# A thinned fold, evictions on another engine and four moved table mends in the prologue of a fused FNet and MLP-Mixer kernel

## Chip, cores and metric

The kernel runs on one core of one Trainium2 chip. The metric is the device time of one execution in microseconds (us), and lower is better.

## The reference

It takes an FFT over the sequence and the features, keeps the real part, and puts an MLP-Mixer behind it (first over tokens, then over channels). Batch 8, sequence 3008, width 256, all float32:

```python
x = np.fft.fft(np.fft.fft(x, axis=1), axis=2).real       # 8 x 3008 x 256
h = np.maximum(x.transpose(0, 2, 1) @ w_tok1, 0.0) @ w_tok2   # 3008 -> 256 -> 3008
u = x + h.transpose(0, 2, 1)
out = u + np.maximum(u @ w_ch1, 0.0) @ w_ch2             # 256 -> 1536 -> 256
```

## The kernel before

It is already tuned: TensorE is fed almost without a gap from batch 1 on, and what follows happens in the first 76 us. There the tables are built, batch 0 goes through its transform, and batch 1 is prepared between batch 0's matmuls. Names that the text needs:

- `xp`, `xm`: rows of x and the mirrored rows. GpSimd issues their loads; the last two of a batch are gathers.
- `fold`: sums and differences of `xp` and `xm` (fold 0 is that of batch 0, fold 1 that of batch 1; tiles `fa`, `fb`, `sab`, `eo`, last `pad`), the input of the transform's first stage `pz` -> `z`. The second stage `pw` -> `w` uses table `td`, then comes `py` -> `yt`.
- tok1 (`pt`, with tables `hp` and `hq`) and tok2 (`pu`, added to `yt` into `ut`): the token part. `pc` -> `c`, `po` or `pa`/`pb` -> `osb`: the channel part, with `s`, sums of `c` that feed `pa` and `pb`. A *slot* is one 128-column block of the first channel product; twelve slots make a chunk of 512 tokens.

GpSimd issues the large loads in program order between its own arithmetic. VectorE does fold 0 and fold 1 and shares the evictions of PSUM with ScalarE. The four *mends* set three columns of `td` right:

```python
    # GpSimd: index columns, the mirror table `anti`, then the weight loads
    for k in range(2):
        ts(ixc[:, k:k + 1], cfeat[:], 128.0 + 0.5 * k, AT.add, 2.0, AT.mult, eng=G)
    # ... tables on VectorE and ScalarE ...
    ts(acol[:], pcol[:], -1.0, AT.mult, 127.0, AT.add, eng=G)
    ts(anti[:], jrow[:, 0:P], acol[:], AT.is_equal, eng=G)

    def load_wc1(k):
        c = slice(HC * k, HC * k + HC)
        for q in range(2):
            gdma(wc1[64 * q:64 * q + 64, 0, c],
                 dram(wc1_t, q * DCH + HC * k, [[2 * DCH, 64], [1, HC]]))
        gather(wc1[:, 1, c], dram(wc1_t, 0, [[HC, 2 * D], [1, HC]]), ixc[:, k:k + 1])

    def load_rest():
        load_wc1(0)
        for th in range(2):
            gdma(w2n[:, th, :], dram(w2_t, th * P * S, [[S, P], [1, S]]))
        load_wc1(1)
        gdma(wc2[:, :, 0:D], dram(wc2_t, 0, [[D, P], [P * D, NCT], [1, D]]))

    # ... the order of the prologue ...
    load_rest()
    fold0 = fold(0, V)
    filler(12)
    take(fold0, 5)                       # first half of fold 0, on VectorE
    ts(ol[:, 0:1], ol[:, 0:1], 2.0, AT.mult)                             # the four mends
    ts(td[:, 0:1], td[:, 64:65], 0.5, AT.mult, ol[:, 0:1], AT.add)
    ts(td[:, 65:66], td[:, 64:65], 0.5, AT.mult, ol[:, 0:1], AT.subtract)
    V.memset(td[:, 64:65], 0.0)
    take(fold0, 5)                       # second half
    # ... front(0) woven with the tables hp, hq (carried) ...
    new_x(1)
    load_xp(1)
    for k in range(2):
        load_xm(1, k)                    # the gathers that fold 1 waits for
```

The main loop, as far as the change touches it:

```python
    own_at = {1: 1, 2: 1, 4: 1, 12: 1, 15: 1, 18: 1, 20: 1, 22: 1, 24: 1, 27: 1, 30: 1, 33: 1,
              36: 1, 39: 1}              # pieces of batch 0's own y and tok2, by slot
    # ... per batch b, chunk c, block ct ...
            on_v = ((1, 5, 8), ())[c] if b == 0 and c < 2 else () if joins else (0, 3, 6, 9)
                slot = NCT * c + ct
                mm1(b, c, c1, ct, on_v)  # evicted by VectorE if ct is in on_v, else ScalarE
                if b == 0:
                    take(own, own_at.get(slot, 0))
                    if 12 <= slot < 30:
                        take(fold1, 1 + slot % 2)
```

Of the kernel before, what the change touches and what calls it, by code (L numbers as in the profile page):

```python
# [12 lines left out]
AT = mybir.AluOpType  # L13
# [23 lines left out]
def kernel(  # L37
# [269 lines left out]

    ts(acol[:], pcol[:], -1.0, AT.mult, 127.0, AT.add, eng=G)
    ts(anti[:], jrow[:, 0:P], acol[:], AT.is_equal, eng=G)
    wc1 = const.tile([P, 2, DCH], FP16, tag="wc1")  # L310
    wc2 = const.tile([P, NCT, D + 1], FP16, tag="wc2")

# [132 lines left out]
    def carried():  # L445
        for dst, t0, t1 in ((hp, tts[0], tts[1]), (hq, tts[2], tts[3])):
            for g2 in range(NG // 2):
                ph = ps_mm("ph")
                for k in range(2):
                    g = 2 * g2 + k  # L450
                    o = ph[:, k * DTOK:(k + 1) * DTOK]
                    nc.tensor.matmul(o, lhsT=t0[:, g * P:g * P + P], rhs=w1p[:, g, :],
                                     start=True, stop=False)
                    nc.tensor.matmul(o, lhsT=t1[:, g * P:g * P + P],
                                     rhs=w1m[:, NG - 1 - g, :],
                                     start=False, stop=True)
                copy(g2 % 2, dst[:, 2 * g2:2 * g2 + 2, :].rearrange("p g k -> p (g k)"),
                     ph[:])
                yield

# [2 lines left out]
    def front(b):  # L463
# [15 lines left out]
        for t0 in (11, 6, 1):  # L479
            for half in range(2):  # L480
                pz = ps_f("pz")
                for k in range(5):
                    stage1(pz[:, 96 * k:96 * k + 96], eo[:, t0 + k], half, t1r, t1m[:])
                zo = z[:, half, :, :].rearrange("p k (u s) -> p u k s", u=4)
                copy(half == 0 and b > 0, zo[:, :, :, t0:t0 + 5],
                     pz[:, 0:480].rearrange("p (t u k) -> p u k t", t=5, u=4))
                yield
        for half in range(2):
# [93 lines left out]
        def tok1():  # L582
            for th in range(2):
                c = slice(th * P, (th + 1) * P)
                pt = ps_f("pt1")
                uv = perb.tile([P, 2, P], FP32, tag="uv", name="uv", bufs=2)
                for o, n, w0, hw in ((0, 129, 0, hp), (129, 127, 130, hq)):
                    if b == 0 and o:
                        sp = perb.tile([P, 129], FP32, tag="sp", name="sp", bufs=1)
                        act(sp[:], pt[:, 0:129])  # L590
                        pt = ps_f("pt2")
                        tt(uv[:, 0, 0:1], sp[:, 0:1], sp[:, P:129], AT.subtract)
                        tt(uv[:, 1, 0:1], sp[:, 0:1], sp[:, P:129], AT.add)
                    for g in range(NG):
                        nc.tensor.matmul(pt[:, o:o + n], lhsT=hw[:, g, c],  # L595
                                         rhs=w[:, g, w0:w0 + n],
                                         start=(g == 0), stop=(g == NG - 1))
                if b == 0:
                    tt(uv[:, 0, 1:], sp[:, 1:P], pt[:, 129:256], AT.subtract)
                    ts(uu[:, th, 0, :], uv[:, 0, :], 0.0, AT.max)  # L600
                    tt(uv[:, 1, 1:], sp[:, 1:P], pt[:, 129:256], AT.add)
                    act(uu[:, th, 1, :], uv[:, 1, :], func=AFT.Relu)
                    yield
                    continue
                sq = perb.tile([P, P], FP32, tag="squ", name="squ", bufs=1)
                act(sq[:], pt[:, P:2 * P])
                tt(uv[:, 0, :], pt[:, 0:P], sq[:], AT.subtract)
                tt(uv[:, 1, :], pt[:, 0:P], sq[:], AT.add)
                ts(uu[:, th, :, :], uv[:], 0.0, AT.max)
                yield  # L610
                if th == 0 and b > 0:
                    yield from rot()

        if b == 0:
            yield from rot()
            yield from y(0)
            yield from tok1()
            y1 = y(1)
            next(y1)
            next(y1)  # L620
            yield
            yield from tok2(0)
            yield from y1
            yield from tok2(1)
            yield from y(2)
            yield from tok2(2)
            for c in (4, 3, 5):
                yield from tok2(c)
        else:
            yield from tok1()  # L630
            for c in range(3):
                yield from y(c)
            for c in (2, 1, 0, 3, 4, 5):
                yield from tok2(c)
# [179 lines left out]
    fold0 = fold(0, V)  # L814
    filler(12)
    take(fold0, 5)
    ts(ol[:, 0:1], ol[:, 0:1], 2.0, AT.mult)
    ts(td[:, 0:1], td[:, 64:65], 0.5, AT.mult, ol[:, 0:1], AT.add)
    ts(td[:, 65:66], td[:, 64:65], 0.5, AT.mult, ol[:, 0:1], AT.subtract)
    V.memset(td[:, 64:65], 0.0)  # L820
    take(fold0, 5)
    own = front(0)
    take(tu_q, 3)
# [16 lines left out]
    for k in range(4):  # L840
# [12 lines left out]
    hold = const.tile([P, 1], FP16, tag="hold")  # L853
    G.memset(sab[:, :, 1, 0:129:128], 0.0)
    own_at = {1: 1, 2: 1, 4: 1, 12: 1, 15: 1, 18: 1, 20: 1, 22: 1, 24: 1, 27: 1, 30: 1, 33: 1,
              36: 1, 39: 1}
    prev = uT = uT_next = None
    folding = left = 0
    for b in range(BB):
        nxt = front(b + 1) if b + 1 < BB else iter(())  # L860
        fold1 = fold(1, V) if b == 0 and BB > 1 else iter(())
        first, done = (24 if b == 0 else 5 + 12 * ((left + 5) // 6 - 1) if left else 0), 0
        for c in range(NCH):
            c1 = work.tile([P, NCT, CW], FP16, tag="c1", name="c1", bufs=2)
            if c == 5 and b % 2:
                G.tensor_copy(out=c1[:, :, 448:512], in_=tail1[:])
            box = {}
            joins = prev is not None and seven(*prev[0:2])
            on_v = ((1, 5, 8), ())[c] if b == 0 and c < 2 else () if joins else (0, 3, 6, 9)
            for ct in range(NCT):  # L870
                slot = NCT * c + ct
                if b == 0 and slot < 3:
                    if slot == 0:
                        mm1(b, c, c1, ct, on_v, range(3))
                else:
                    mm1(b, c, c1, ct, on_v)
                if b == 0 and slot in (4, 16):
                    uT = turn_u(b, c)
                if ct == (11 if b == 0 and c == 1 else 10) and (b, c) not in ((0, 0), (BB - 1, NCH - 1)):
                    uT_next = turn_u(*divmod(NCH * b + c + 1, NCH))  # L880
                if joins:
                    if ct in places:
                        mm2_seven(*prev, places[ct], pbox)
                    if ct in sum_at:
                        sums(prev[2], pbox, sum_at[ct])
                elif prev is not None and ct % 3 == 2:
                    mm2(*prev, ct // 3, pbox)
                if slot == 1 and b == 0:
                    weight_sums()
                if b == 0:  # L890
                    take(own, own_at.get(slot, 0))
                    if 12 <= slot < 30:
                        take(fold1, 1 + slot % 2)
                    if slot == 29 and BB > 2:
                        load_x(2)
                    if 30 <= slot < 34:
                        th, hb = (slot - 30) // 2, slot % 2
                        G.tensor_copy(out=w2r[:, th, 32 * hb:32 * hb + 32, 0:NQ],
                                      in_=w2v[0][:, th, 32 * hb:32 * hb + 32, :])
                while done < NFRONT * (slot + 1 - first) // (71 - first):  # L900
                    take(nxt, 1)
                    done += 1
                if ct == 5 and (left or done >= 8):
                    if not left and folding < b + 2 < BB:
                        folding, left, fold2 = b + 2, NFOLD, fold(b + 2, G)
                    if left:
                        if joins:
                            G.tensor_copy(out=hold[:], in_=pbox[3][:, 0, 0, 0:1])  # L908
                        n = min(left, 6 if c == 5 or b < 2 else 5)
                        take(fold2, n)  # L910
                        left -= n
                        if left == 0 and folding + 1 < BB:
                            load_x(folding + 1)
            if c == 5 and b % 2 == 0:
                G.tensor_copy(out=tail1[:], in_=c1[:, :, 384:448])
            prev, pbox, uT = (b, c, c1, uT), box, uT_next
# [32 lines left out]
```

## Time and profile before

| | before |
|---|---|
| median of 3 runs, us | 601.67 (601.45 to 602.59) |
| span of the profiled run, us | 599.8 |
| TensorE busy / VectorE / ScalarE / GpSimd | 97% / 75% / 65% / 43% |
| TensorE stalls by start distances (how they are found is told in the prediction), us | 12.8 |

The prediction below reads this profile at length. GpSimd's timeline of the prologue (start, duration, engine, line, operation, output and inputs, count; in brackets the idle time before it and what ended it):

```profile
13.03 0.34 POOL L86 TENSOR_SCALAR ixc<-cfeat 128x1 int32<-128x1 f32 x2
13.43 0.19 POOL L86 TENSOR_SCALAR acol<-pcol 128x1 f32<-128x1 f32 x1
13.72 1.45 POOL L84 TENSOR_SCALAR anti<-jrow,acol 128x128 f16<-128x128 f32 x1
15.12 1.17 POOL L106 DMA_DIRECT2D wc<-in_moe_w_ch_dram  x2
...
26.24 0.96 POOL L109 DMA_INDIRECT xm<-in_x_dram,ix  x1 [2.65 <-DMA w2n<-in_moe_w_tok_dram]
```

Second, one row of the table by stretch (window; length; busy time and count of PE, PEld, DVE, ACT, POOL; clock; DMA share; GB/s), for the 4 us in which the loads issued from 15 us on take over from the earlier ones:

```profile
19.00:23.00 4.00, 3.56 (x38) 2.58 (x38) 2.98 (x7) 3.45 (x9) 3.43 (x5) 1.00 1.13 208
```

### The profile page before, as it was taken

The numbers are of one execution on the slowest core, as the hardware profiler recorded it, in microseconds if no ns is written. First come the engines' busy times: TensorE is split into PE (matmuls) and PEld (weight loads), VectorE is DVE, ScalarE is ACT, GpSimd is POOL, SyncE is SP. The second block draws the span as 40 slices with busy tenths as digits, with TensorE's granted clock in tenths as the row PEclk, the third lists the DMA queues.
The fourth block names the chain that finished last, engine by engine and source line by source line (L and its number), as shares of the span: only waits on it lengthen the run. The fifth ranks groups of instructions, "written<-read, shape, count | busy, mean of one in ns | idle before, by whom it ended". The sixth has DMA issues, their size and how long they took to land.

```text
span 599.8 us, 15331 instructions
## 1 busy us (share of the span) xinstructions
PE 582.5 (97%) x6273; PEld 417.8 (70%) x6273; DVE 449.5 (75%) x924; ACT 390.2 (65%) x753; POOL 255.1 (43%) x396
## 2 busy tenths in 40 slices
PE   3899999999999999999999999999999999999997
PEld 3756676677767776667767777677766777666776
DVE  8769879685898668766898668856688757966663
ACT  8764665478647865477656867568665786556662
POOL 8550545937555554626348444565555000000000
PEclk9999999999999999999999999999999999999999
DMA  8992822277138913394335753376133422323533
GB/s 158 207 192 61 170 50 53 61 149 119 37 71 121 149 37 68 78 181 54 68 84 91 135 89 55 67 147 113 37 60 80 93 55 55 77 61 77 93 72 88
DMA packets 83414, 55.69 MB, mean 93 GB/s; under 512 B 53778, under 2 KB 80082, under 8 KB 82578
## 3 DMA queue, kind: packets, MB, share of 16 engines
q1 hardware_dynamic: 76816, 36.82, 31.9%
q0 software_dynamic: 6208, 17.63, 16.2%
q8 instruction: 49, 0.80, 0.6%
q10 hardware_dynamic: 320, 0.26, 0.2%
q14 instruction: 21, 0.17, 0.1%
HBM read 35.26 MB, written 24.64 MB: 100 GB/s over the span
## 4 chain that ended last, share of the span: by engine, by line
PE 82%; DVE 1%; issue 0%; DVEq 0%
PE pc L662 36%; PE pa L712 17%; PE pb L712 13%; PE pu L566 6%; PE po L775 4%; PE pt L595 3%; PE pz L471 1%; PE py L538 1%; PE pw L512 1%; PE pw L508 1%; DVE s L90 1%; DVE osb L90 0%; DVE ut L90 0%; PE pz L496 0%; DVE q L90 0%
## 5 line engine op out<-in xcount | busy, mean ns | idle before, releaser
L97 ACT ACTIVATE c<-pc 128x512 f16<-128x512 f32 (+1 forms) x553 | 314.4, 591 | 156.2 <-PE pc L662 138.7
L662 PE MATMUL pc<-ut,wc 128*128 128x512 f16 (+1 forms) x1152 | 316.5, 374 | 1.2 <-DVE ut L90 1.2
L712 PEld LDWEIGHTS <-s 128*128 128x128 f16 x1968 | 123.5, 98 | 37.5 <-DVE s L90 0.6
L662 PEld LDWEIGHTS <-wc 128*128 128x128 f16 x1152 | 97.0, 98 | 50.7 <-issue 3.0
L712 PEld LDWEIGHTS <-c 128*128 128x128 f16 x1476 | 93.0, 97 | 27.8
L90 DVE TENSOR_TENSOR q<-pa,uT 128x256 f32<-128x256 f32 x123 | 52.5, 427 | 47.6 <-PE pa L712 47.5
L90 DVE TENSOR_TENSOR s<-c 128x1536 f16<-128x1536 f16 x82 | 80.7, 984 | 4.7 <-ACT c L97 4.7
L908 POOL COPY hold<-s 128x1 f16<-128x1 f16 x29 | 5.4, 187 | 173.5 <-DVE s L90 173.5
L90 DVE TENSOR_TENSOR osb<-pb,q 128x256 f32<-128x256 f32 x123 | 52.0, 422 | 23.8 <-PE pb L712 20.3
L90 DVE TENSOR_TENSOR ut<-pu,yt 128x512 f16<-128x512 f32 (+1 forms) x96 | 63.3, 672 | 0.8 <-PE pu L566 0.4
L90 POOL TENSOR_TENSOR eo<-sab 96x512 f16<-96x512 f16 x48 | 52.7, 1114 | 1.6
L566 PE MATMUL pu<-w2r,uu 128*128 128x512 f16 (+1 forms) x168 | 50.0, 379 | 0.3 <-DVE ut L90 0.3
L90 POOL TENSOR_TENSOR sab<-fa,fb 96x256 f16<-96x256 f16 (+1 forms) x72 | 46.7, 673 | 0.0
L90 DVE TENSOR_TENSOR s<-s,c 128x1536 f16<-128x1536 f16 x41 | 40.4, 986 | 0.0
L97 ACT ACTIVATE w<-pw 128x257 f16<-128x257 f32 x90 | 34.8, 387 | 8.4 <-PE pw L512 5.5
L90 DVE TENSOR_TENSOR s<-c,s 128x1536 f16<-128x1536 f16 x41 | 39.0, 952 | 0.0
L775 PE MATMUL po<-wc,c 128*128 128x256 f16 x288 | 35.4, 273 | 0.0
L712 PE MATMUL pb<-wc,c 128*128 128x128 f16 x492 | 34.4, 219 | 0.0
L712 PE MATMUL pa<-wc,c 128*128 128x128 f16 x492 | 34.4, 219 | 0.0
L712 PE MATMUL pa<-t2w,s 128*128 128x128 f16 x492 | 34.2, 219 | 0.1
L712 PE MATMUL pb<-t1w,s 128*128 128x128 f16 x492 | 34.2, 219 | 0.0
L712 PE MATMUL pa<-t4w,c 128*128 128x128 f16 x492 | 34.2, 219 | 0.0
(187 smaller groups left out, 728.0 us busy)
## 6 DMA issues: line engine op xcount, KB each, us to landing
out_dram<-osb SPq DMA_DIRECT2D x83, 256.0 KB
xp<-in_x_dram POOLq DMA_DIRECT2D x14, 408.0 KB, 6.4
out_dram<-osb SPq DMA_DIRECT2D x11, 192.0 KB
uT<-ut SPq DMA_TRANSPOSE x96
w2n<-in_moe_w_tok_dram POOLq DMA_DIRECT2D x2, 752.0 KB, 9.8
w1p<-in_moe_w_tok_dram POOLq DMA_DIRECT2D x2, 384.0 KB, 8.2
wc<-in_moe_w_ch_dram POOLq DMA_DIRECT2D x1, 768.0 KB, 15.3
xp<-in_x_dram POOLq DMA_DIRECT2D x2, 272.0 KB, 5.7
```

The lines of the kernel that those rows point to most:

```text
L90: eng.tensor_tensor(out=out_, in0=a, in1=b, op=op)
L97: nc.scalar.activation(out=out_, in_=in_, func=func, scale=scale, **kw)
L471: nc.tensor.matmul(out_, lhsT=rows[:, half * P:half * P + P], rhs=tab, start=True, stop=True)
L508: nc.tensor.matmul(pw[:, 0:256].rearrange("p (h d) -> p h d", h=2)[:, :, 0:65], lhsT=zg[:, 0, g], rhs=td[:, 0:130].rearrange("p (h d) -> p ...
L512: nc.tensor.matmul(pw[:, 64:322].rearrange("p (h d) -> p h d", h=2)[:, :, 0:64], lhsT=zg[:, 1, g], rhs=td[:, 130:258].rearrange("p (h d) - ...
L538: nc.tensor.matmul(py[:, P * k:P * k + P], lhsT=w[:, 4 * c + k, o:o + P], rhs=tab[:, 4 * c + k, :], start=True, stop=True)
L566: nc.tensor.matmul(pu[:, 0:64 * nk], lhsT=uu[:, th, h, :], rhs=w2[:, th, :, 8 * c:8 * c + nk], start=(th == 0), stop=(th == 1))
L595: nc.tensor.matmul(pt[:, o:o + n], lhsT=hw[:, g, c], rhs=w[:, g, w0:w0 + n], start=(g == 0), stop=(g == NG - 1))
L662: nc.tensor.matmul(pc[:, 0:n], lhsT=wc1[:, h, ct * P:(ct + 1) * P], rhs=ut[:, c, h, 0:n], start=(h == 0), stop=(h == 1))
L712: nc.tensor.matmul(dst[:, P * a:P * a + P], lhsT=left[:, k, a, :], rhs=right[:, k, :], start=(first and k + a == 0), stop=(k == NH - 1), s ...
L775: nc.tensor.matmul(po[:, o:o + D], lhsT=c1[:, ct, ks * P:ks * P + P], rhs=wc2[:, ct, 0:D], start=(ct == 0), stop=(ct == NCT - 1))
L908: G.tensor_copy(out=hold[:], in_=pbox[3][:, 0, 0, 0:1])
```

## The change

The intent is to take work off VectorE where it is late: the mends go to GpSimd, one `hq` copy and seven evictions go to ScalarE, fold 1 is spread thinner in slots 12 to 20, and the last pieces of tok2 come one and two slots earlier. The lines in full, but for the unchanged context:

```diff
     ts(anti[:], jrow[:, 0:P], acol[:], AT.is_equal, eng=G)
+    ts(ol[:, 0:1], ol[:, 0:1], 2.0, AT.mult, eng=G)
+    ts(td[:, 0:1], td[:, 64:65], 0.5, AT.mult, ol[:, 0:1], AT.add, eng=G)
+    ts(td[:, 65:66], td[:, 64:65], 0.5, AT.mult, ol[:, 0:1], AT.subtract, eng=G)
+    G.memset(td[:, 64:65], 0.0)
@@ tables hp and hq
-                copy(g2 % 2, dst[:, 2 * g2:2 * g2 + 2, :].rearrange("p g k -> p (g k)"),
+                copy(g2 in ((1, 3, 5) if dst is hp else (1, 5)),
+                     dst[:, 2 * g2:2 * g2 + 2, :].rearrange("p g k -> p (g k)"),
                      ph[:])
@@ evictions of z
-                copy(half == 0 and b > 0, zo[:, :, :, t0:t0 + 5],
+                copy(half == 0 and b > 1, zo[:, :, :, t0:t0 + 5],
@@ tok1
-                pt = ps_f("pt1")
+                pt = ps_f("pt1") if b else ps_mm("pt1")
@@ front of batch 0
-            yield from y(0)
-            yield from tok1()
+            y0, t1 = y(0), tok1()
+            for piece in (y0, y0, y0, t1, t1):
+                next(piece)
+                yield
@@ prologue
     take(fold0, 5)
-    ts(ol[:, 0:1], ol[:, 0:1], 2.0, AT.mult)
-    ts(td[:, 0:1], td[:, 64:65], 0.5, AT.mult, ol[:, 0:1], AT.add)
-    ts(td[:, 65:66], td[:, 64:65], 0.5, AT.mult, ol[:, 0:1], AT.subtract)
-    V.memset(td[:, 64:65], 0.0)
     take(fold0, 5)
@@ main loop
-              36: 1, 39: 1}
+              35: 1, 37: 1}
-        first, done = (24 if b == 0 else 5 + 12 * ((left + 5) // 6 - 1) if left else 0), 0
+        first, done = (25 if b == 0 else 5 + 12 * ((left + 5) // 6 - 1) if left else 0), 0
-            on_v = ((1, 5, 8), ())[c] if b == 0 and c < 2 else () if joins else (0, 3, 6, 9)
+            on_v = ((1, 5, 8), (), ())[c] if b == 0 and c < 3 else () if joins else (0, 3, 6, 9)
-                        take(fold1, 1 + slot % 2)
+                        take(fold1, 1 if slot < 21 else 2)
```

## The prediction

> **What bounds the kernel now.** I read the page's busy shares first, then the table of busy time by stretch, then the chain of waits and the timeline of the first 80 us.
>
> ```profile
> PE 582.5 (97%) x6273; PEld 417.8 (70%) x6273; DVE 449.5 (75%) x924; ACT 390.2 (65%) x753; POOL 255.1 (43%) x396
> ```
>
> ```profile
> 34.00:42.00 8.00, 8.00 (x44) 3.91 (x42) 4.54 (x8) 6.07 (x12) 5.03 (x5) 1.00 1.09 211
> 42.00:50.00 8.00, 8.00 (x56) 5.12 (x55) 7.74 (x22) 4.53 (x10) 2.29 (x2) 1.00 0.62 66
> 50.00:54.00 4.00, 3.10 (x20) 1.85 (x19) 4.00 (x13) 1.02 (x2) 0.00 (x0) 1.00 0.00 1
> 54.00:62.00 8.00, 8.00 (x73) 5.18 (x70) 8.00 (x28) 3.89 (x7) 0.45 (x1) 1.00 0.42 99
> 76.00:590.00 514.00, 513.59 (x5645) 369.99 (x5644) 383.21 (x723) 338.70 (x652) 216.50 (x335) 1.00 0.43 83
> ```
>
> The columns are window, length, then busy time of PE, PEld, DVE, ACT, POOL, granted clock, DMA share, GB/s. TensorE is the bound from 76 to 590 us; only the prologue has slack, and from 50 to 62 us it is VectorE that is full (12.00 of 12 us) while ScalarE works 4.91.
>
> How much is there to win? In the chain, matmuls with nothing to wait for start at fixed distances: 0.216 us for 512 columns, 0.056 for 128. Summing such distances over all 6,273 matmuls I get 574.8 us of pure TensorE work. The first matmul starts at 8.06, the end comes about 4.2 us after the last start, so 12.8 us of the 599.8 are stalls, nearly all before 76 us. The change aims at these:
>
> ```profile
> 12.82 0.14 DVE L84 TENSOR_SCALAR ol<-ol 128x1 f32<-128x1 f32 x1
> ...
> 13.45 0.71 DVE L90 TENSOR_TENSOR fa<-xp,xm 96x1016 f16<-96x1016 f16 x1
> ...
> 16.02 0.93 PE L476 MATMUL pz<-t1n,eo 96*128 96x96 f16 x11 [1.19 <-DVE eo L90]
> ```
>
> ```profile
> 29.98 0.28 PE L595 MATMUL pt<-w,hq 128*128 128x127 f16 x2 [0.19 <-DVE hq L101]
> ```
>
> ```profile
> 42.12 0.77 DVE L90 TENSOR_TENSOR fa<-xp,xm 96x508 f16<-96x508 f16 x1 [2.67 <-DMA xm<-in_x_dram,ix]
> 42.81 1.76 DVE L90 TENSOR_TENSOR fb<-xm,xp 96x508 f16<-96x508 f16 x1
> ...
> 52.41 0.68 DVE L90 TENSOR_TENSOR ut<-pu,yt 128x512 f16<-128x512 f32 x1
> ```
>
> ```profile
> 53.14 0.38 PE L662 MATMUL pc<-ut,wc 128*128 128x512 f16 x1 [0.90 <-DVE ut L90]
> ...
> 62.34 0.20 PE L496 MATMUL pz<-t1n,pad 96*128 96x24 f16 x2 [0.26 <-DVE pad L90]
> ```
>
> ```profile
> 68.48 3.08 DVE L90 TENSOR_TENSOR s<-c 128x1536 f16<-128x1536 f16 x1
> ...
> 72.15 0.64 PE L566 MATMUL pu<-w2n,uu 128*128 128x448 f16 x2 [0.42 <-DVE ut L90]
> ```
>
> The bracket understates a stall, since a matmul's end is modelled; by start distances the five cost 1.35, 0.36, 1.06, 0.42 and 0.59 us. In each VectorE is late: four tiny mends sit ahead of the second half of fold 0; the copies of hq run to the last; fold 1, held by a transfer until 42.12, stands ahead of ut; fold 1's last piece (pad) is late; and s takes 3.08 us where its kind takes about 0.98.
>
> **What the Trainium skill says.** "Perfetto Trace Analysis", Identifying the Most-Contended Engine: matmul busy share is no measure of headroom. The trace agrees: 97% is shown also where starts are stretched, which is why I count start distances. "ScalarE: Activation LUTs", What ACT_TABLE_LOAD costs: an ACTIVATE with immediates takes 186 + 0.833 N ns, neighbours overlapping by about 93; for N = 512 and 480 that is 612 and 586 ns. The trace has 601 (c) and 610 to 850 (z, three of them), and 680 and 695 for the same on VectorE, so moved evictions get no dearer. "SBUF — State Buffer", Who interferes with whom: a VectorE instruction with two SBUF inputs and a GpSimd one that reads SBUF block each other. The trace agrees: fb took 1.76 us instead of 0.41 beside GpSimd's t4w, and the 3.08 us s lay beside GpSimd's copies of w2r (65.17 to 70.75) and ended 0.81 after them.
>
> **The change, part by part.** The instruction orders of the two builds show what moved. TensorE's order differs in one thing: the two halves of the last tok2 piece (448 columns) stand in slots 35 and 37 instead of 36 and 39 (a slot is one 128-column block of the first channel product). The changes of `first` and of the y/tok1 interleave leave every order as it was; they are worth nothing.
>
> 1. Mends to GpSimd. VectorE goes from eo straight to fa, at 12.82 instead of 13.45. The second xm of batch 0 landed at 12.34 in the trace, so no transfer holds it. Gain 0.63. Does it carry? ScalarE's z copies start at 16.95 after 0.82 us of idleness, so at 16.32, and the second stage (19.86, behind ScalarE) at 19.23. There the mirrored w1 rows landed at 18.33, 19.33 and 19.66, and are now wanted at 19.58: up to 0.1 lost. GpSimd does the mends after anti (ends 15.17), three at about 0.3 and a memset, so by about 16.4; needed at 19.2. Its weight loads are issued about 1 us later, but transfers run at 200 to 220 GB/s without a gap from 5 to 42 us, so they land when they did.
>
> 2. hq. One copy goes from VectorE to ScalarE. VectorE's last one then starts after yt at 28.64, ends about 29.3, before TensorE wants it at 29.62: the 0.36 goes. The tok1 result in another PSUM group waits for the fourth hq copy, on ScalarE done by about 28.35, when it is wanted at 28.37: nothing lost. Parts 1 and 2: about 0.95 at the first pc.
>
> 3. Fold 1 thinned to slot 20. VectorE cannot start before 42.12 whatever happens, since that transfer is bandwidth bound. So I lay the new order end to end from there with the old start distances: fa 0.69, fb 1.69 (GpSimd beside it), ends 0.11, four sums 1.00, eo 0.34, osb 0.73, eo 0.34, yt 1.20, fa, fb, ends 0.78, ut 0.60, four sums 0.94, eo 0.34: the second ut starts at 50.88, ends 51.5. TensorE, 0.95 ahead, would be there at 51.13 and starts at 51.55 instead of 53.14. So far 1.6; the stall shrinks from 1.06 to 0.4 and is now set by the transfer at 42.
>
> 4. Evictions to ScalarE. In slots 24 to 35, 4 c (0.68) and 3 z (0.70) leave VectorE, 4.8 us, while 4 thinned pieces (about 1.7) come in. From 51.48: eo pieces, two fold blocks of 2.4, two osb (0.73), two ut (0.60) and the last two pieces reach pad at about 60.15. TensorE, 1.6 ahead, wants it at 61.92 - 1.59 = 60.33: the 0.42 goes. Total 2.0. ScalarE then has c and z in each of slots 25 to 30, about 0.50 + 0.65 = 1.15 us, where slots 25 to 30 took 53.88 to 61.48, 1.27 each: it fits, with three PSUM buffers for slack.
>
> 5. Last tok2 in slots 35 and 37. Its first ut now precedes the slow s, but the second stands behind s, q and the next s, and the PSUM buffer it holds is wanted in slot 40. GpSimd's load of x waits for fold 1 and moves up 2.2 us, with TensorE, so s ends as before relative to it; I lay the wait at about 0.6, as the 0.59 was. Nothing gained.
>
> Sum: 0.63 + 0.36 - 0.05, then 0.65 and 0.4: 2.0 us, 0.33% of the time. 601.67 - 2.0 = 599.7; I say 599.8 for small new stalls after 76 us, where PSUM buffers fall differently.
>
> **The rivals.** First, ScalarE becomes the bound in slots 25 to 30: for it, one z took 0.85, so 1.35 per slot, above 1.27; against it, its 4.91 of 12 us now. If so, 0.5 to 1.5 us of parts 3 and 4 are lost: 600.3 to 601.2. Second, the mends hurt on GpSimd, by blocking fold 0's sums or by late weight loads: for it, fb's 1.76; against it, five tiny GpSimd instructions lay beside fold 0's first three sums, 1.10 us, and the second three without them took 1.09. Then 0.6 less at the start, but as the transfer at 42.12 sets part 3, only about 0.1 to 0.5 is lost in the end: about 600.1. Third, slot 40's new wait exceeds the old by s's length: 1 us more, 600.7. Fourth, it goes better: if s slips past GpSimd's copies, 0.6 more, 599.1.
>
> **Range and chances.** A change that can touch at most 3.8 us of stalls, 0.6%, cannot reach 2%; a loss of 12 us would need a stall in every batch, and the order from batch 2 on is the same. Three runs of before span 1.1 us, so noise is about half of the gain. Range 598.7 to 601.3. Chances: faster 0.01, within 2% 0.98, slower 0.01.
>
> **What would show it.** Right: the second fold-0 fa near 12.8, the pz wait down from 1.19 to about 0.6, no wait of pt on hq, fa of fold 1 still at about 42.1, the second ut starting near 50.9, no wait on pad, VectorE below full from 54 to 62 and ScalarE above 6 of 8 us there. Wrong: fold 1's first fa later than 42.5 (then GpSimd's delay did reach the transfers), pc waiting on ScalarE's c, or a wait above 1 us near slot 40. A steady stretch (76 to 590) that changes by more than 0.5 us would break the whole reading.

## The result, and the profile after

| | before | after |
|---|---|---|
| median, us | 601.67 (601.45 to 602.59) | 601.64 (601.61 to 601.65) |
| span of the profiled run, us | 599.8 | 599.7 |
| stalls by start distances, us | 12.8 | 12.7 |

The ratio after to before is 0.9996, 95% interval 0.9973 to 1.0018: the same. A ratio here is the mean time of one kernel's runs over the mean time of the other's of the same rounds, so it is not quite the ratio of the medians. A second set of six runs on another chip gave 601.33 against 601.44, ratio 0.9998 (0.9986 to 1.001). The predicted 599.8 with its range up to 601.3 did not hold. All outputs are right.

The busy shares of the page after moved as the change meant them to, away from VectorE (449.5 to 443.8 us) and to ScalarE (390.2 to 394.5):

```profile
PE 582.5 (97%) x6273; PEld 417.9 (70%) x6273; DVE 443.8 (74%) x912; ACT 394.5 (66%) x761; POOL 257.8 (43%) x400
```

The table by stretch, after:

```profile
19.00:23.00 4.00, 3.43 (x34) 2.54 (x34) 3.05 (x7) 3.24 (x8) 3.70 (x6) 1.00 0.98 146
...
50.00:54.00 4.00, 2.52 (x18) 1.50 (x17) 3.96 (x13) 0.89 (x2) 0.00 (x0) 1.00 0.00 1
54.00:62.00 8.00, 8.00 (x73) 5.34 (x72) 7.90 (x35) 6.64 (x13) 0.86 (x2) 1.00 0.42 99
76.00:590.00 514.00, 513.43 (x5646) 369.91 (x5645) 382.86 (x722) 338.50 (x652) 216.62 (x334) 1.00 0.43 83
```

From 76 us on nothing changed (513.43 us of TensorE work against 513.59). From 50 to 54 us TensorE works *less* than before, 2.52 against 3.10 us. And from 19 to 23 us the transfers move 146 GB/s where they moved 208. GpSimd's timeline after shows what is new ahead of that dip:

```profile
13.08 1.30 POOL L86 TENSOR_SCALAR ixc<-cfeat 128x1 int32<-128x1 f32 x2
...
15.84 0.22 POOL L84 TENSOR_SCALAR ol<-ol 128x1 f32<-128x1 f32 x1
16.17 0.55 POOL L86 TENSOR_SCALAR td<-td,ol 128x1 f16<-128x1 f16 x2
16.78 0.11 POOL L313 MEMSET td<- 128x1 f16 x1
17.02 1.17 POOL L106 DMA_DIRECT2D wc<-in_moe_w_ch_dram  x2
...
27.89 0.95 POOL L109 DMA_INDIRECT xm<-in_x_dram,ix  x1 [2.64 <-DMA w2n<-in_moe_w_tok_dram]
```

The first weight load is issued at 17.02 instead of 15.12. Of these 1.9 us, 17.02 - 15.84 = 1.18 are the mends. The rest, some 0.7, comes from what else the move does: without the mends VectorE enters the second half of fold 0 at 13.04 instead of 13.45, and GpSimd's two `ixc` instructions beside its `fa` and `fb` take 1.30 us instead of 0.34 (`acol` 0.40 instead of 0.19; `anti`, which lay beside `fa` and `fb` before, 0.93 instead of 1.45). The gather of batch 1 is issued at 27.89 instead of 26.24, 1.65 later, again behind the landing of `w2n`. The packets of GpSimd's queue, added up in each trace, show that the delay arises in the dip and then stays: the first 3 MB are through at 18.21 us before and 18.36 after, the first 3.4 MB at 20.23 and 21.31, the first 7 MB at 38.06 and 39.57. VectorE's timeline shows where that arrives:

```profile
13.04 0.69 DVE L90 TENSOR_TENSOR fa<-xp,xm 96x1016 f16<-96x1016 f16 x1
...
44.04 0.50 DVE L90 TENSOR_TENSOR fa<-xp,xm 96x508 f16<-96x508 f16 x1 [5.09 <-DMA xm<-in_x_dram,ix]
...
52.50 0.68 DVE L90 TENSOR_TENSOR ut<-pu,yt 128x512 f16<-128x512 f32 x1
...
72.28 0.61 DVE L90 TENSOR_TENSOR ut<-pu,yt 128x448 f16<-128x448 f32 x1
```

Fold 1 starts at 44.04 instead of 42.12, after 5.09 us of idleness. It takes less time from there to the second `ut` (8.46 us against 52.41 - 42.12 = 10.29), but it starts so late that `ut` starts at 52.50, where it was 52.41. TensorE, after:

```profile
15.53 0.22 PE L481 MATMUL pz<-t1n,eo 96*128 96x96 f16 x1 [0.64 <-DVE eo L90]
...
53.23 0.38 PE L669 MATMUL pc<-ut,wc 128*128 128x512 f16 x1 [1.48 <-DVE ut L90]
...
72.94 0.22 PE L513 MATMUL pw<-td,z 128*128 128x130 f16 x1 [0.53 <-DVE ut L90]
```

The wait for fold 0 fell from 1.19 to 0.64; those for `hq` and `pad` are gone; the one for `ut` rose from 0.90 to 1.48. Comparing the same matmul in both traces turns this into an account of how far after is ahead:

| TensorE at | before | after | after is ahead by |
|---|---|---|---|
| first `pz` of the second half of fold 0 | 16.02 | 15.53 | 0.49 |
| first `pw` of the second stage | 19.86 | 19.46 | 0.40 |
| first `pc` | 33.63 | 33.12 | 0.51 |
| `pc` on the second `ut` of the third chunk | 53.14 | 53.23 | -0.09 |
| first matmul on `pad` | 62.34 | 62.01 | 0.33 |
| end of the span | 599.8 | 599.7 | 0.1 |

The gain is there, is lost at 53 us (0.60), is won back in part at `pad`, and shrinks to nothing in small waits behind it: the wait near slot 40 is 0.69 by start distances where its predecessor was 0.59, and one at 133 us is 0.31 where it was 0.17.

### The profile page after: what moved, and what is told of

Same layout as the page of the kernel before. It is cut to its first block, busy times and chain, and to the rows that moved or that the text cites. A ratio compares the mean times of both kernels' runs of the same rounds, so it can differ in the third digit from the quotient of the medians. Undisturbed runs are those within 1.5% of the kernel's fastest.

```text
span 599.7 us, 15334 instructions
## 1 busy us (share of the span) xinstructions
PE 582.5 (97%) x6273; PEld 417.9 (70%) x6273; DVE 443.8 (74%) x912; ACT 394.5 (66%) x761; POOL 257.8 (43%) x400
## 3 DMA queue, kind: packets, MB, share of 16 engines
q0 software_dynamic: 6208, 17.63, 16.7%
HBM read 35.26 MB, written 24.64 MB: 100 GB/s over the span
## 4 chain that ended last, share of the span: by engine, by line
PE 82%; DVE 1%; issue 0%; DVEq 0%
PE pc L669 36%; PE pa L719 17%; PE pb L719 13%; PE pu L571 6%; PE po L782 4%; PE pt L600 3%; PE pz L476 1%; PE py L543 1%; PE pw L517 1%; PE pw L513 1%; DVE s L90 1%; DVE osb L90 0%; DVE ut L90 0%; DVE z L101 0%; PE pz L501 0%
```

## The experiments

The theory after this reading: the mends hold GpSimd up just before it issues the weight loads; the transfer queue runs short at 19 to 23 us; all loads behind land later; fold 1 starts later and the third chunk waits. The rivals are that the moved instructions themselves hurt (mends slow VectorE's fold, evictions fill ScalarE, thinning delays something), or that the gain was never there. In the dose table further down all kernels stand side by side. "M" means median.

### a: only the mends undone

After, with the four mends back on VectorE between the halves of fold 0; everything else of the change stays.

```diff
-    ts(ol...), ts(td...), ts(td...), G.memset(td...)      # on GpSimd behind anti
     take(fold0, 5)
+    ts(ol[:, 0:1], ol[:, 0:1], 2.0, AT.mult)
+    ts(td[:, 0:1], td[:, 64:65], 0.5, AT.mult, ol[:, 0:1], AT.add)
+    ts(td[:, 65:66], td[:, 64:65], 0.5, AT.mult, ol[:, 0:1], AT.subtract)
+    V.memset(td[:, 64:65], 0.0)
     take(fold0, 5)
```

> The changed kernel with the four mends back on VectorE between the halves of fold 0, all else kept. Theory T (the mends on GpSimd delay the issue of the first weight loads, 15.12 to 17.02 us, the transfers run short from 19 to 23 us, and the x rows of fold 1 land 1.75 us later): first load issued near 15.1, first fa of fold 1 near 42.1, the stall of pc before the third chunk under 0.6 us (1.65 in the changed kernel), time 599.8 to 600.4. Rival R1 (the late landing is chance, or thinning and evictions gain nothing): fa near 44 or the stall still above 1 us, time 601.3 to 601.9. Rival R2 (GpSimd is late because VectorE's fold 0 starts sooner and blocks it, not because of the mends) expects here the same as T.

Measured: M 600.18 (599.99 to 600.48), ratio to before 0.9968 (0.9955 to 0.9981). This kernel gives up the 0.49 us at fold 0 and is nevertheless 1.5 us faster than after. Its stretch row, and VectorE's timeline:

```profile
19.00:23.00 4.00, 3.45 (x38) 2.47 (x38) 3.09 (x7) 3.45 (x9) 3.38 (x6) 1.00 1.12 208
```

```profile
41.90 0.83 DVE L90 TENSOR_TENSOR fa<-xp,xm 96x508 f16<-96x508 f16 x1 [2.23 <-DMA xm<-in_x_dram,ix]
...
51.01 0.68 DVE L90 TENSOR_TENSOR ut<-pu,yt 128x512 f16<-128x512 f32 x1
```

The dip is gone, fold 1 starts at 41.90, and the second `ut` at 51.01, where the prediction had laid it at 50.88. No TensorE row from 50 to 75 us has a wait. So the rest of the change does what was predicted, and what cancels it comes with the move of the mends (with their time on GpSimd or with the earlier fold 0; d tells these apart).

### b: only the mends moved

Before, with nothing but the mends moved to GpSimd behind `anti`.

```diff
     ts(anti[:], jrow[:, 0:P], acol[:], AT.is_equal, eng=G)
+    ts(ol...), ts(td...), ts(td...), G.memset(td...)      # eng=G
@@
     take(fold0, 5)
-    ts(ol...), ts(td...), ts(td...), V.memset(td...)
     take(fold0, 5)
```

> The kernel before with only the mends moved to GpSimd. T: first load issued at 16.3 to 17.0, first fa of fold 1 at 43.3 to 44.1, and with the old dense fold ahead of ut the stall of pc grows from 1.06 to 2.3 to 3.3 us although TensorE is up to 0.5 us ahead there; time 602.8 to 603.6. R1: fa near 42.1, time 601.2 to 601.8. R2: as T.

Measured: M 603.99 (602.21 to 607.81, six runs), ratio 1.0035 (1.0009 to 1.0061), so slower than before, and with a scatter of 5.6 us. The direction is the theory's; the size is above what was expected. In the traced run, one of its slower ones (605.91), the first weight load was issued at 17.48, the transfers ran at 140 GB/s from 19 to 23 us, and fold 1 started only at 46.12. That is more than the bytes missed in the dip explain ((208 - 140) GB/s by 4 us is 272 KB, 1.3 us at 208 GB/s). By its packets the queue was 2.0 us late at 7 MB (40.07 against 38.06); the other 2 us arose in the last step, the landing of the gather, and why was not found.

### c: the mends on GpSimd, but behind the first two loads

```diff
         for q in range(2):
             gdma(wc1[64 * q:64 * q + 64, 0, c], ...)
+        if k == 0:
+            ts(ol...), ts(td...), ts(td...), G.memset(td...)   # eng=G
         gather(wc1[:, 1, c], ...)
```

> The changed kernel with the mends kept on GpSimd but behind the first two weight loads. T: first load issued near 15.8, no dip of the transfer rate under 190 GB/s for more than 1 us from 19 to 23 us, first fa of fold 1 at 42.1 to 42.8, time 599.5 to 600.3. R1: 601.3 to 601.9. R2: the load is still late by the blocking alone; fa near 43.7, time near 601.5.

Measured: M 600.66 (599.99 to 601.87), ratio 0.9978 (0.9963 to 0.9993). The same four instructions on the same engine, beside the same VectorE work, cost about 1 us less when two loads go out ahead of them. By the times alone this is not quite clear of noise (the interval overlaps with that of the second set of after, 0.9986 to 1.001), but the queue was 1.0 us late at 7 MB, where after's was 1.5. The median is a little above the range expected, since the delay is moved to the gather (issued at 18.40, where before has 16.59) and not removed: the stretch from 19 to 23 us ran at 173 GB/s, between 208 and 146, and not above 190 as expected.

### d: the mends on VectorE, but behind all of fold 0

```diff
     take(fold0, 5)
     take(fold0, 5)
+    ts(ol...), ts(td...), ts(td...), V.memset(td...)
```

> The changed kernel with the mends on VectorE but behind fold 0, in its 0.77 us of idleness at 16.8 us: fold 0 as early as in the changed kernel, GpSimd without mends. T: first load issued near 15.8 (only the blocking by fold 0, about 0.7), fa of fold 1 at 42.1 to 42.8, TensorE about 0.4 ahead from the start, time 599.4 to 600.2. R2: fa near 43.7 as in the changed kernel, time near 601.5. R1: 601.3 to 601.9.

Measured: M 600.40 (600.07 to 600.54), ratio 0.9969 (0.9956 to 0.9982). It has the early fold 0 of after and no mends on GpSimd, and so parts the 1.9 us of delay into their two causes: `ixc` took 1.24 us here too, and the first load was issued at 15.87, 0.75 later than before without any mend in the way. The transfers nonetheless ran at 214 GB/s from 19 to 23 us. So 0.75 us of delay leaves the queue full, and 1.9 does not. Fold 1 started at 42.78, within what was expected. The time is 0.2 above the expectation and no better than a: TensorE keeps a wait of 0.23 us for `ut` in the third chunk, and a gain at fold 0 is of no use as long as the third chunk hangs on a transfer.

### e: d, and four idle instructions on GpSimd in place of the mends

```diff
     ts(anti[:], jrow[:, 0:P], acol[:], AT.is_equal, eng=G)
+    ts(scs[:], pcol[:], 2.0, AT.mult, eng=G)
+    ts(scr[:, 0:1], anti[:, 64:65], 0.5, AT.mult, scs[:], AT.add, eng=G)
+    ts(scr[:, 65:66], anti[:, 64:65], 0.5, AT.mult, scs[:], AT.subtract, eng=G)
+    G.memset(scr[:, 64:65], 0.0)
```

> The kernel with the mends on VectorE behind fold 0 (600.4 us, fa of fold 1 at 42.8), plus four idle instructions of the mends' shapes on GpSimd, into a scratch tile that nobody reads, in the place that the mends have in the changed kernel. Theory T (GpSimd's time ahead of the loads costs, nothing else): first load at about 17.0, transfer rate dipping below 170 GB/s from 19 to 23 us, fa of fold 1 at 43.6 to 44.3, the stall of pc back at 1.2 to 1.9 us, time 601.2 to 602.2. Rival R3 (it is the mends' own dependence, the second stage waiting for the table): as without the idle ones, fa at 42.3 to 42.9, 600.1 to 600.6 us.

The mends could hurt through what waits for `td`, rather than by occupying GpSimd; idle instructions of the same shapes, whose result nobody reads, tell these apart. Measured: M 601.61 (600.57 to 606.23, six runs), ratio 1.0005 (0.9976 to 1.0034). The loss against d, 1.2 us by the medians on the same chip (0.9 if the medians of before in the two sets, 602.06 and 601.71, are taken off), comes back with instructions that nobody waits for, so it is the occupied GpSimd. All six runs lie above all five of d, the fastest only just. The trace is no clean witness: it fell on the fastest of the six runs (600.57). The first load was issued at 17.14 and the transfers ran at 137 GB/s, as the theory has it, but fold 1 started at 42.88, outside the 43.6 to 44.3 that were expected, no wait for `ut` shows in the third chunk, and that run lost nothing against d's traced one (600.54). Its queue was late all the same, by 1.5 us at 7 MB (39.53); only the gather's last step was quick.

### f, g, h: a without one of the other parts

With the mends out of the way, each other part was undone alone, on a's base. These ran in e's set, where the median of before was 602.06 and not 601.71 as in a's, so distances from a by medians may be some 0.35 us too large; the ratios to before allow for that.

f, fold 1 not thinned:

```diff
-                        take(fold1, 1 if slot < 21 else 2)
+                        take(fold1, 1 + slot % 2)
```

> The kernel with the mends back between the halves (600.2 us) without the thinning, evictions kept on ScalarE. If VectorE's order is what thinning buys: the second ut starts near 52.2 instead of 50.7, pc stalls 0.6 to 0.9 us, no wait on pad; time 600.8 to 601.3. If thinning buys nothing: 600.0 to 600.5.

Measured: M 601.26 (601.01 to 601.61), ratio 0.998 (0.9963 to 0.9998), 1.1 above a by the medians (0.7 by the ratios), within what was expected. The wait of the third chunk returns, on TensorE at `53.69` with 1.19 us, above the 0.6 to 0.9 that were expected, since more of fold 1 stands ahead of `ut` again.

g, evictions of `z` and of the third chunk's `c` back on VectorE:

```diff
-                copy(half == 0 and b > 1, zo[:, :, :, t0:t0 + 5],
+                copy(half == 0 and b > 0, zo[:, :, :, t0:t0 + 5],
@@
-            on_v = ((1, 5, 8), (), ())[c] if b == 0 and c < 3 else ...
+            on_v = ((1, 5, 8), ())[c] if b == 0 and c < 2 else ...
```

> The same kernel without the moved evictions (c of the third chunk and z of batch 1 as before), thinning kept. VectorE never pauses from 42 us to pad and thinning only reorders its work, so pad comes at about 62.1 as in the kernel before and TensorE, wanting it near 61.1, stalls about 1 us: time 601.0 to 601.6. If the evictions buy nothing: 600.0 to 600.5. If thinning without them is worth all of it: 600.2 as well.

Measured: M 603.12 (602.49 to 603.5), ratio 1.0011 (0.9993 to 1.0029). That is 2.9 us above a (2.6 by the ratios), and more than expected. TensorE's timeline shows three waits on VectorE before 64 us, one of them by `pad`, which thinning has put off:

```profile
57.74 0.37 PE L472 MATMUL pz<-t1n,eo 96*128 96x96 f16 x5 [0.22 <-DVE z L101]
...
60.67 0.39 PE L472 MATMUL pz<-t1n,eo 96*128 96x96 f16 x5 [0.79 <-DVE eo L90]
...
63.10 0.39 PE L497 MATMUL pz<-t1n,pad 96*128 96x24 f16 x2 [0.44 <-DVE pad L90]
```

So thinning without the evictions gains nothing over before (the interval holds 1), while the evictions without thinning (f) keep part of the gain. VectorE hardly pauses there (busy 3.96 us from 50 to 54 and 7.90 of 8 from 54 to 62): thinning only reorders its work, and the likely reading is that a later fold then collides with the evictions. A kernel with neither part on a's base was not run, so how much each is worth alone is not shown.

h, the `hq` copy back on VectorE and `pt1` in its old PSUM group:

```diff
-                copy(g2 in ((1, 3, 5) if dst is hp else (1, 5)), dst...
+                copy(g2 % 2, dst...
@@
-                pt = ps_f("pt1") if b else ps_mm("pt1")
+                pt = ps_f("pt1")
```

> The same kernel without the move of one hq copy and of the tok1 result to the other PSUM group. In its trace pc of the third chunk does not stall, so TensorE sets that point and the 0.36 us before pt on hq should come back in full: time 600.4 to 600.8. If VectorE's fold still sets it: 600.0 to 600.3.

Measured: M 600.61 (600.25 to 600.98, and one run at 604.31), ratio 0.998 (0.9954 to 1.0006): 0.4 above a by the medians, within what was expected, but small beside the interval; against before of its own set it is as good as a to 0.1 us (601.71 - 600.18 = 1.53 and 602.06 - 600.61 = 1.45). So its times do not show that the part gains. Its trace shows that the wait on `hq` is back (0.35 us by start distances, at 30.78).

### After once more, and twice the dose

The next four ran on another chip, so after itself ran again as their yardstick.

> The changed kernel itself once more, in the rounds of its variants. T: first load at 17.0, rate near 146 GB/s from 19 to 23 us, fa of fold 1 at 42.8 to 44.3 depending on the run, time 601.0 to 602.2 and more scatter than a kernel whose loads are issued by 16 us. If its late fa was chance: time 600.0 to 600.6.

Measured: M 601.33 (600.6 to 602.39), as expected. First load at 17.37, 134 GB/s, fold 1 at 43.56. In this trace the wait for the second `ut` is only 0.20 us, because TensorE itself came later (first `pc` at 34.02 and not 33.12); the second `ut` still set the start of that `pc`, at 52.84.

i is d with eight idle instructions (e's four, twice).

```diff
     ts(anti[:], jrow[:, 0:P], acol[:], AT.is_equal, eng=G)
+    # e's four instructions, twice
```

> The kernel with the mends on VectorE behind fold 0 and twice the idle instructions on GpSimd (eight). T: first load at about 18.2, rate from 19 to 23 us at 80 to 130 GB/s, fa of fold 1 at 44 to 46, time 602.5 to 604, about twice the cost of the four (1.2 us by the medians). If the cost saturates or the four's cost was chance: 600.4 to 601.8.

Measured: M 601.53 (601.38 to 602.75), ratio 1.0002 (0.9989 to 1.0015). The expectation of 602.5 to 604 was missed. The trace shows why the dose was smaller than meant: the first load was issued at 18.03, only 0.66 after after_again's, since the second four took 0.9 us. The transfer rate fell on, to 118 GB/s, but fold 1 started at 44.00, 0.44 later, and then:

```profile
53.12 0.38 PE L675 MATMUL pc<-ut,wc 128*128 128x512 f16 x1 [1.18 <-DVE ut L90]
```

So the wait is there, of after's size and not doubled. The delay of the queue did grow with the delay of the issue, to 2.1 us at 7 MB (40.14, against 39.53 in e and 39.57 in after_again); the time did not grow in proportion.

### j: the first two loads ahead even of `anti`

d, with `acol` and `anti` moved behind the first two loads as well. If late issue costs time, early issue should cure it.

```diff
-    ts(acol[:], pcol[:], -1.0, AT.mult, 127.0, AT.add, eng=G)
-    ts(anti[:], jrow[:, 0:P], acol[:], AT.is_equal, eng=G)
@@ load_wc1, behind its two gdma
+        if k == 0:
+            ts(acol[:], pcol[:], -1.0, AT.mult, 127.0, AT.add, eng=G)
+            ts(anti[:], jrow[:, 0:P], acol[:], AT.is_equal, eng=G)
```

> The kernel with the mends on VectorE behind fold 0 (600.4 us) and on GpSimd the first two weight loads ahead of acol and anti. T: first load at about 14.5, no dip, fa of fold 1 at 41.7 to 42.4, fold 0 early, TensorE 0.4 ahead at the start: time 599.6 to 600.2. If anti comes too late for TensorE (wanted near 16.7): 600.3 to 600.9.

Measured: M 600.04 (599.82 to 600.27), ratio 0.9971 (0.9959 to 0.9984), as expected. First load at 14.25; fold 1 started at 42.70, not within the 41.7 to 42.4 that were expected. It is 1.3 faster than after on the same chip, and no faster than a or d relative to before: once the queue was full, an earlier issue won nothing here. Two waits are left in its trace, 0.67 us for `ut` in the third chunk and 0.51 near slot 40.

### k: j, and the last pieces of tok2 in slots 34 and 35

This aims at the wait near slot 40, for a `ut` that stands behind a slow `s`.

```diff
-              35: 1, 37: 1}
+              34: 1, 35: 1}
```

> The same with the last tok2 halves in slots 34 and 35, both ahead of the slow s on VectorE. The wait of pw for the second ut in slot 40 (0.7 us in the changed kernel) should go, if no other wait takes its place: 0.1 to 0.7 us less than the kernel with the loads first, 599.2 to 600.0. If the slow s only moves the wait to the product of s: no gain.

Measured: M 599.22 (599.17 to 599.8), ratio to before 0.9961 (0.9948 to 0.9974); the fastest kernel here, 2.2 us below before and 2.1 below after on the same chip. VectorE's timeline:

```profile
42.17 0.74 DVE L90 TENSOR_TENSOR fa<-xp,xm 96x508 f16<-96x508 f16 x1 [3.22 <-DMA xm<-in_x_dram,ix]
...
50.87 0.68 DVE L90 TENSOR_TENSOR ut<-pu,yt 128x512 f16<-128x512 f32 x1
...
67.00 0.61 DVE L90 TENSOR_TENSOR ut<-pu,yt 128x448 f16<-128x448 f32 x1
67.53 1.98 DVE L90 TENSOR_TENSOR s<-c 128x1536 f16<-128x1536 f16 x1
```

The second `ut` starts at 50.87, the prediction's 50.88; the last 448-column `ut` stands ahead of `s`; and no TensorE row from 50 to 75 us has a wait. Its stalls add up to 9.5 us by start distances, against 12.8 before and 12.7 after (its first matmul also starts 0.75 us later than before's, at 8.81, so the span is only 2.6 us shorter). Not all of the step from j is the slots: in the traced runs fold 1 also started 0.53 us sooner than in j, with the same prologue, and how much of the 0.8 us between the medians belongs to which was not separated.

### All doses side by side

Each row is the traced run of one kernel, sorted by when GpSimd issued the first `wc` load. "7 MB" is when the first 7 MB had passed through GpSimd's queue, added up from the packets of the trace. "Spread" is the highest less the lowest of all its runs.

| kernel | first load, us | GB/s, 19 to 23 us | 7 MB, us | fold 1 starts, us | median / ratio to before | spread, us |
|---|---|---|---|---|---|---|
| j | 14.25 | 194 | 38.37 | 42.70 | 600.04 / 0.9971 | 0.5 |
| k | 14.51 | 213 | 38.23 | 42.17 | 599.22 / 0.9961 | 0.6 |
| before | 15.12 | 208 | 38.06 | 42.12 | 601.67 / 1 | 1.1 (3 runs) |
| a | 15.39 | 208 | 38.12 | 41.90 | 600.18 / 0.9968 | 0.5 |
| f (no thinning) | 15.41 | 201 | 38.41 | 42.75 | 601.26 / 0.998 | 0.6 |
| g (no evictions) | 15.42 | 205 | 38.49 | 42.70 | 603.12 / 1.0011 | 1.0 |
| h (no `hq` copy) | 15.66 | 210 | 38.06 | 41.73 | 600.61 / 0.998 | 4.1 |
| d | 15.87 | 214 | 38.20 | 42.78 | 600.40 / 0.9969 | 0.5 |
| c (gather at 18.40) | 16.01 | 173 | 39.04 | 42.66 | 600.66 / 0.9978 | 1.9 |
| after | 17.02 | 146 | 39.57 | 44.04 | 601.64 / 0.9996 | 0.04 (3 runs) |
| e | 17.14 | 137 | 39.53 | 42.88 | 601.61 / 1.0005 | 5.7 |
| after, again | 17.37 | 134 | 39.57 | 43.56 | 601.33 / 0.9998 | 1.8 |
| b (before's other parts) | 17.48 | 140 | 40.07 | 46.12 | 603.99 / 1.0035 | 5.6 |
| i | 18.03 | 118 | 40.14 | 44.00 | 601.53 / 1.0002 | 1.4 |

There is an edge between 16 and 17 us. Loads issued by 15.9 leave the rate at 194 to 214 GB/s; those issued from 17.0 on let it fall to 118 to 146. The queue reaches 7 MB by 38.5 us in the first group, at 39.0 in c and at 39.5 or later in all of the second, where at 3 MB all 14 traces still lie between 18.2 and 18.5 us. Fold 1 starts by 42.8 in the first group and in c, and in the second at 43.6 or later except in e. The last load issued ahead of these is the third part of `w1m`, which landed at 19.66 in the trace of before; it appears that a load issued at 17 has too little lead to take over without a hole.

## Why the prediction was wrong

**The step that failed** is in part 1: "Its weight loads are issued about 1 us later, but transfers run at 200 to 220 GB/s without a gap from 5 to 42 us, so they land when they did." The rate was read rightly as a mean (203 to 208 GB/s; single microseconds lie between 172 and 260) and shows that the transfers were busy; it does not show that the queue has a microsecond in hand. The load was issued 1.9 us later, not 1, the stretch from 19 to 23 us fell to 146 GB/s, which is (208 - 146) GB/s by 4 us = 248 KB or 1.2 us at 208 GB/s, the queue was 1.5 us late at 7 MB, and fold 1 started 1.92 us later. The premise of part 3, "VectorE cannot start before 42.12 whatever happens", was true, but only bounds from one side. Experiments a, c and d each make that issue earlier again in another way, with all else of fold 1 left as it is, and e makes it late with instructions that nobody waits for; the time goes with the issue in all four, and so does the queue in their traces (7 MB at 38.1, 39.0, 38.2 and 39.5 us), though in e's traced run alone fold 1 was not late.

**The delay itself, 1.9 us and not 1.** The mends were put at about 1.2 us ("by about 16.4" after 15.17) and took 1.18. What was left out is the second effect: an earlier fold 0 slides onto GpSimd's `ixc`, which goes from 0.34 to 1.30 us. d shows it alone (0.75 late). The prediction had looked for this contention and found none, but it looked at VectorE's sums (1.10 against 1.09 us) and not at GpSimd's own instructions, which paid. The sign stood in the trace of before: `anti` took 1.45 us there beside `fa` and `fb`, and 0.63 in j, where it lay beside smaller work.

**Rival two, and its size.** Rival two was this: "the mends hurt on GpSimd, by blocking fold 0's sums or by late weight loads". It was sized at "0.1 to 0.5" us, "about 600.1". Its second half is what happened, at 1.5 us (after less a). The signpost was right as well: "fold 1's first fa later than 42.5".

Term by term, in us:

| term | predicted | measured |
|---|---|---|
| fold 0 sooner | 0.63 | 0.49 |
| mirrored `w1` rows late | -0.05 | -0.22 |
| on the way from `pz` to `pw` | 0 | -0.09 |
| `hq` wait gone | 0.36 | 0.31 |
| third chunk's wait | 0.65 | -0.60 |
| `pad` wait gone | 0.4 | 0.42 |
| last tok2, slot 40 | 0 | -0.10 |
| small wait at 133 us | -0.1 | -0.14 |
| sum | 1.9 | 0.1 |

The third chunk alone is 1.25 of the 1.8 us missed. (The prediction's 0.1 for small stalls behind 76 us stands outside its sum of 2.0; both columns are rounded.)

- **Fold 0**: VectorE started `fa` at 13.04, not 12.82. In before, 0.97 us lay between the start of the last sums and `fa` (12.48 to 13.45), in after 0.51 (12.53 to 13.04): 0.46 saved, not 0.63.
- **`hq`**: right; no wait on `hq` or on `pt1`'s PSUM buffer is in the trace; what the part is worth in time, h does not show clear of noise.
- **Fold 1 laid end to end**: right. From its start to the second `ut` it took 8.46 us after and 9.11 in a, against 8.76 laid out; in k the start was 50.87 against 50.88. Only the origin was wrong, and one small sum: from the start of that `ut` to its `pc` it is 0.73 us in before (52.41 to 53.14), so 50.88 leads to 51.61 and not 51.55.
- **Evictions**: right. ScalarE works 6.64 of 8 us from 54 to 62 ("above 6"), and no `pc` waits for its copies. The copies of `c` took 590 ns on average in after (54 to 62 us) and those of `z` 676; the prediction's 612 and 586 are estimates from the formula in "ScalarE: Activation LUTs", What ACT_TABLE_LOAD costs. VectorE is below full, but barely: 7.90 of 8. That the order needs the evictions was not said; g shows it (2.9 us above a by the medians).
- **Slot 40**: right as laid: 0.69 against about 0.6. That other slots could take this wait away was not seen; in k it is gone.
- **76 to 590 us unchanged**: right, 513.43 against 513.59.

**Open.** What decides the last step, from the queue's progress to the landing of the gather. At 7 MB e, after and after_again agree to 0.04 us, yet fold 1 started at 42.88, 44.04 and 43.56; in b it took 2 us more than the delay of its queue. In b's trace, from 44 to 47 us, the packets of SyncE's queue (the transposes of `ut`) hold the 16 engines for most of the time (152% of it as the profile counts packets, against 9.5% for GpSimd's queue), so the last packets of the gather may be waiting behind them; no run tests this. Also open are why twice the dose (i) did not cost more, and the scatter. The landing of x varies from run to run without any change: the first `fa` of fold 0, which waits for a transfer too in most of them, started anywhere from 10.01 to 10.69 in the traced runs. The kernels with a late issue scatter by 1.4 to 5.7 us in their sets of five or six (after's first three runs agree to 0.04), a, d, f, g, j and k, with an early one, by 0.5 to 1.0, h apart with its one run at 604.31. A queue without reserve would fit this, but no run shows it, and two things count against it: before itself, with an early issue, spread by 1.4 to 3.0 us in its sets of eleven, and the longest runs of b (607.81), e (606.23) and h (604.31) have a mean granted clock of 0.994, 0.994 and 0.997, where most others have 0.999 or 1.000. A clock lower by 0.6% is worth up to 3.6 us of 600 (an estimate), so part of the scatter may be the clock's.

## What to carry to other kernels

An engine that also issues transfers is not idle because its busy share is low: ask how long ahead of the end of the previous load it issues the next one, and read the rate in the few microseconds where one takes over from the other, not over the whole stage. Where instructions must go on such an engine, put them behind the issues, not ahead. A new order may pay only when work has also been moved off the full engine, so test each alone and both.

## What the Trainium skill lacked or had wrong

- "SBUF — State Buffer", Who interferes with whom, says that a VectorE instruction with two SBUF inputs contends with a GpSimd one that reads SBUF. This agrees, and here GpSimd paid: its two tiny `ixc` instructions took 1.30 us beside VectorE's `fa` and `fb` (0.34 otherwise), while these kept their 0.69 and 0.68 us. What the page lacks is the consequence that mattered here. It tells of loads held up because their descriptors cannot be written; in d it was GpSimd's arithmetic ahead of the loads that was held up, and the first of them was issued 0.75 us later.
- "DMA: Bandwidth & Descriptors", Bandwidth, Measured, has no row for loads that convert the type, nor for many loads queued one behind the other. The loads of the prologue (96 to 768 KB each, some strided or gathered) turn float32 into float16, and the profile's rate counts the float16 bytes: GpSimd's queue moved 17.63 MB in the execution of before, and 35.26 MB were read from HBM, just twice as much. They moved 198 to 203 GB/s from 5 to 19 us and 202 to 209 from 23 to 42 us, so about 400 GB/s were read (an estimate from this factor of two). Set beside a figure for loads without conversion, the profile's rate would look like half of what was read.
- No page has a figure for the lead that GpSimd needs to keep a queue full. Here loads issued by 15.9 us kept 194 to 214 GB/s, and from 17.0 us on 118 to 146, where the last load ahead of them landed at 19.66 in the trace of before (19.72 to 20.06 in the three others that record it). If 19.66 is taken for all of them, a lead of 3.8 us was enough and 2.6 was not (an estimate from these numbers).
